# A smaller set-up product, a divided last store and later softmax steps in a TensorE-bound kernel

## The chip, the cores and the metric

The kernel runs on one core of one Trainium2 chip. The metric is the device time of one execution in microseconds (us), given as the median of several runs. The profile covers one execution; its "span", from the first to the last instruction, is some 1.8 us shorter than the metric.

## The reference

A dynamic convolution (7 taps, weights by softmax from `weight_gen`, 8 heads) is followed by a maxout layer:

```python
# attention part: x (8, 4160, 192), weight_gen (8, 4160, 8 heads, 7 taps)
w = softmax(weight_gen, axis=-1)                  # with a padded window of 7 tokens
out = einsum('bshk,bskhg->bshg', w, x_unfolded)   # -> (33280, 192)
# maxout part, w1 and w2 (192, 1024), w_out (1024, 192)
g = np.maximum(x @ w1, x @ w2)
return g @ w_out                                  # float32
```

## The kernel before

The kernel uses max(h1, h2) = h1 + relu(h2 - h1). So the output is `y @ (w1 @ w_out) + relu(y @ (w2 - w1)) @ w_out`. The small matrix `w10 = w1 @ w_out` (192 x 192) is computed once at the start, on the chip: w1 is transposed on TensorE (`tp`), copied to SBUF (`w1t`), multiplied by `wo` (`pw`), and copied to `w10`. Two output columns share 384 transposed rows, that is three slices of 128, so `w10` is kept in three slices: rows 0 to 127, rows 64 to 191, and rows 128 to 191 followed by 0 to 63.

The parts that the change touches (cuts marked):

```python
w1t = pstage.tile([P, FCH * 256], BF16, name="w1t")
def w1_transposed():
    tp = ...
    for fi in range(FCH):                                   # 8 blocks, 3 transposes each
        for at, kind, nr in ((0, "E", P), (P + 64, "E", 64), (P, "T", 64)):
            nc.tensor.matmul(tp[:, fi * 256 + at:...], lhsT=w1[kind][...], rhs=ident[...], is_transpose=True, ...)
    for h in range(2):
        nc.scalar.copy(out=w1t[:, h * 1024:(h + 1) * 1024], in_=tp[:, h * 1024:(h + 1) * 1024])
...
def w10_product():
    pw = ...
    for k in range(3):                                      # 3 x 8 products of 192 columns
        for fi in range(FCH):
            nc.tensor.matmul(pw[:, k * 256:k * 256 + D],
                lhsT=w1t[:, fi * 256 + 64 * k:fi * 256 + 64 * k + P], rhs=wo[:, fi * D:(fi + 1) * D], ...)
    nc.scalar.copy(out=_sub(w10, 0, [[D, 3], [1, D]]), in_=_sub(pw, 0, [[256, 3], [1, D]]))
...
hidden(1); w1_transposed(); ln(1); shift(1)                 # order of issue in the set-up (cut)
hidden(2); weights(1, 0); weights(1, 4); ...; exp_sum(2); sum_transpose(2); ...
hidden(3); w10_product(); sum_transpose(3); ...; out_rests(3, 0)    # out_rests uses w10 first (L275)
```

The last pair of output columns is copied from PSUM by one ScalarE instruction of 384 columns (line 305) and stored by one transfer (line 312). In the steady part, `extra(t)` issues ln, exponentials (`weights`, `exp_sum`), VectorE's multiplications and additions at fixed tiles of a batch of 16. At the very start, until its first data arrive, TensorE runs 115 warm-up products (`warm`, line 504) whose result nobody uses.

The softmax here doesn't subtract the row's maximum and nothing guards it: scores larger than these inputs give would overflow.

Of the kernel before, what the change touches and what calls it, by code (L numbers as in the profile page):

```python
# [10 lines left out]
BF16 = mybir.dt.bfloat16  # L11
# [6 lines left out]
def _sub(base: bass.AP, off: int, dims):  # L18
    ap = [list(base.ap[0])] + [[int(s), int(c)] for s, c in dims]
    return dataclasses.replace(base, offset=base.offset + off, ap=ap)  # L20
# [3 lines left out]
def kernel(  # L24
# [9 lines left out]
    nc = tc.nc  # L34

    B, S, D = x.shape
    H, K = weight_gen.shape[2], weight_gen.shape[3]
    F = moe_w1.shape[1]
    P = 128
    PAD = K - 1  # L40
    WGC = H * K
    FCH = F // P
    CPP = B * S // P
# [6 lines left out]
    NB = len(BATCHES)  # L50


    def pieces(b):
        n = BATCHES[b][1]
        at, done = [], 0
        for w in {0: (4, 4, 4, 4), 1: (4, 4, 8)}.get(b, (8, 8) if n == 16 else (n,)):
            at.append((done, w))
            done += w
        return at
# [8 lines left out]
    NT = len(TILES)  # L68
# [54 lines left out]
    def exp_sum(b):  # L123
        e_ts[b] = pe_.tile([P, BATCHES[b][1] * WGC], FP32, name="e_t", tag="e")
        nc.scalar.activation(out=e_ts[b], in_=wg_ts[b], func=AF.Exp)  # L125

    def red(b):
        TH = BATCHES[b][1] * H
        s_ts[b] = psm.tile([P, TH], FP32, name="sum_t", tag="sum")
        nc.vector.reduce_sum(out=s_ts[b], in_=_sub(e_ts.pop(b), 0, [[K, TH], [1, K]]), axis=AX.X)  # L130

    def ln(b):
        nc.scalar.activation(out=s_ts[b], in_=s_ts[b], func=AF.Ln)

    def shift(b):
        TH = BATCHES[b][1] * H
        w_t = _sub(wg_ts[b], 0, [[K, TH], [1, K]])
        nc.vector.tensor_tensor(out=w_t, in0=w_t, in1=_sub(s_ts.pop(b), 0, [[1, TH], [0, K]]),
                                op=ALU.subtract)

    def weights(b, o):

        N = dict(pieces(b))[o] * H
        if b not in en_ts:
            en_ts[b] = pen.tile([P, 16 * WGC * 2], BF16, name="en_t", tag="en")
        nc.scalar.activation(  # L146
            out=_sub(en_ts[b], o * WGC * 2, [[2 * N, K], [2, N], [1, 2]]),
            in_=_sub(wg_ts[b], o * WGC, [[1, K], [K, N], [0, 2]]), func=AF.Exp,
        )


    def mul(b, o):

        n = dict(pieces(b))[o]
        if b not in m_ts:
            m_ts[b] = pm.tile([P, K * 16 * D], BF16, name="m_t", tag="m")
        nc.vector.tensor_tensor(  # L157
            out=m_ts[b][:, K * o * D:K * (o + n) * D],
            in0=_sub(xb_ts[b], o * D, [[D, K], [1, n * D]]),
            in1=_sub(en_ts[b], o * WGC * 2, [[2, K * n * H], [0, G // 2], [1, 2]]),  # L160
            op=ALU.mult,
        )

    def adds(b, o):

        w = dict(pieces(b))[o]
        n = w * D
        m_t = m_ts[b]

        def taps(at, step, cnt):  # L170
            return _sub(m_t, K * o * D + at * n, [[step * n, cnt], [1, w * D]])

        if b not in y_ts:
            y_ts[b] = py.tile([P, 16 * D], BF16, name="y_t", tag="y")
        nc.vector.tensor_tensor(out=taps(0, 1, 3), in0=taps(0, 1, 3), in1=taps(3, 1, 3), op=ALU.add)  # L175
        nc.vector.tensor_tensor(out=taps(0, 2, 2), in0=taps(0, 2, 2), in1=taps(1, 5, 2), op=ALU.add)  # L176
        nc.vector.tensor_tensor(out=y_ts[b][:, o * D:(o + w) * D],  # L177
                                in0=taps(0, 1, 1), in1=taps(2, 1, 1), op=ALU.add)

    def transpose(u):  # L180

        b, o, n = UNITS[u]
        yt = pyt.tile([P, 8 // 2 * 3 * P], BF16, name="yt", tag="yt")
        nc.sync.dma_start_transpose(
            out=yt[:, 0:n // 2 * 3 * P].rearrange("p (b t) -> p b t", t=P),
            in_=y_ts[b][:, o * D:(o + n) * D],
        )
        yt_ts[u] = yt

        c = b + 1 if o == 0 else b + 2  # L190
        if u > 5 and c < NB:
            nc.gpsimd.tensor_copy(out=gate, in_=yt[:, 0:1])  # L192
            if o == 8:
                load_x(c, 0, min(8, BATCHES[c][1]))
            else:
                if BATCHES[c][1] > 8:
                    load_x(c, 8, BATCHES[c][1] - 8)
                if b + 3 < NB:
                    load_wg(b + 3, nc.gpsimd)
# [18 lines left out]
    rd_at, hd_at, op_at, o_t = {}, {}, {}, []  # L218
# [40 lines left out]
    def column(c):  # L259

        b = min(c // 16, NB - 1)
        for u, (ub, o, n) in enumerate(UNITS):
            if ub == b and o <= c - BATCHES[b][0] < o + n:
                k = c - BATCHES[b][0] - o
                return u, k // 2, k % 2
# [32 lines left out]
    def evac(p, n):  # L298

        tile_, at = op_at[p]  # L300
        k = 2 * p % 24
        m = min(n, 12 - k // 2)
        for q, w in ((0, m), (m, n - m)):
            if w:
                nc.scalar.copy(out=_sub(o_t[0], (k + 2 * q) % 24 * D, [[2 * D, w], [D, 2], [1, D]]),  # L305
                               in_=_sub(tile_, at + q * D, [[D, w], [512, 2], [1, D]]))
        for q in range(p, p + n):
            u, i, _ = column(2 * q)
            w = 1 if u == NU - 1 else UNITS[u][2] // 2
            if i % w == w - 1:  # L310
                k = 2 * (q + 1 - w)
                nc.scalar.dma_start(
                    out=bass.AP(tensor=out.tensor, offset=k * D, ap=[[CPP * D, P], [1, 2 * w * D]]),
                    in_=o_t[0][:, k % 24 * D:(k % 24 + 2 * w) * D],
                )
# [3 lines left out]
    OUTS, c = [], 0  # L319
# [73 lines left out]
    w10 = consts.tile([P, 3 * D], BF16, name="w10")  # L393
# [5 lines left out]
    with tc.tile_pool(name="pstage", bufs=1) as pstage:  # L399
# [7 lines left out]
        for p0, p1, eng in ((16, P, nc.sync), (1, 16, nc.gpsimd)):  # L407
            eng.dma_start(
                out=xs[p0:p1, 0:PAD * D],
                in_=bass.AP(tensor=x.tensor, offset=(p0 * CPP - PAD) * D,  # L410
                            ap=[[CPP * D, p1 - p0], [1, PAD * D]]),
# [38 lines left out]
        for o in (0, 4, 8, 12):  # L450
            weights(0, o)
        nc.vector.tensor_copy(out=xb_ts[0][:, PAD * D:(PAD + 4) * D],
                              in_=xs[:, PAD * D:(PAD + 4) * D])
# [5 lines left out]
        def w_diff(h, copy):  # L459
# [15 lines left out]
            out=wo[:, :].rearrange("p (f d) -> p f d", d=D),  # L475
            in_=bass.AP(tensor=moe_w_out.tensor, offset=0, ap=[[D, P], [P * D, FCH], [1, D]]),
# [3 lines left out]
        load_x(1, 8, 8)  # L480
        load_wg(3, nc.gpsimd)

        w1t = pstage.tile([P, FCH * 256], BF16, name="w1t")

        def w1_transposed():

            tp = ps["o"].tile([P, 1024], FP32, name="tp", tag="op")[:, :].bitcast(BF16)
            for fi in range(FCH):
                for at, kind, nr in ((0, "E", P), (P + 64, "E", 64), (P, "T", 64)):
                    nc.tensor.matmul(  # L490
                        tp[:, fi * 256 + at:fi * 256 + at + nr],
                        lhsT=w1[kind][0:nr, fi * P:(fi + 1) * P],
                        rhs=ident[0:nr, 0:nr], is_transpose=True, skip_group_check=True,
                    )
            for h in range(2):
                nc.scalar.copy(out=w1t[:, h * 1024:(h + 1) * 1024],
                               in_=tp[:, h * 1024:(h + 1) * 1024])

        warm = ps["h"].tile([P, 1024], FP32, name="warm", tag="hd")

# [27 lines left out]
        def w10_product():  # L528

            pw = ps["o"].tile([P, 1024], FP32, name="pw", tag="op")  # L530
            for k in range(3):
                for fi in range(FCH):
                    nc.tensor.matmul(  # L533
                        pw[:, k * 256:k * 256 + D],
                        lhsT=w1t[:, fi * 256 + 64 * k:fi * 256 + 64 * k + P],
                        rhs=wo[:, fi * D:(fi + 1) * D],
                        start=(fi == 0), stop=(fi == FCH - 1), skip_group_check=True,
                    )
            nc.scalar.copy(out=_sub(w10, 0, [[D, 3], [1, D]]), in_=_sub(pw, 0, [[256, 3], [1, D]]))


        hidden(2)
# [37 lines left out]
    def extra(t):  # L580

        u, k = TILES[t]
        b, o, n = UNITS[u]
        s = o + k
        if s == 0 and b + 1 < NB:

            c = b + 1
            if c + 1 < NB:
                red(c + 1)
            mul(c, 0)  # L590
            adds(c, 0)
        if s == 1 and b + 2 < NB:
            ln(b + 2)
            shift(b + 2)
            mul(b + 1, 8)
            adds(b + 1, 8)
        if k == 2 and 6 < u + 1 < NU:
            transpose(u + 1)
        if b + 2 < NB:
            for o, at in zip((o for o, _ in pieces(b + 2)), (12, 15)):  # L600
                if s == at:
                    weights(b + 2, o)
        if s == 9 and b + 3 < NB:
            exp_sum(b + 3)

    for g in range(3, len(OUTS)):
        if GROUPS[min(g, len(GROUPS) - 1)][1] == 3 and "c" not in ps:
# [51 lines left out]
```

## Time and profile before

| | before |
|---|---|
| time, first three runs | 428.1 us (427.99 to 428.15) |
| span of the profiled execution | 425.9 us (this execution took 427.68 us) |
| first hidden product (line 237) | 15.15 us |
| first use of `w10` (line 275) | 32.93 us, 17.78 after it |
| end of the last product of TensorE | 422.13 us |
| from there to the end | 3.76 us |

Read it as three lengths: a start that ends with the first hidden product, a body that TensorE fills almost without a gap, and a tail of copy, store and final checks. The body is 422.13 - 15.15 = 406.98 us. Any gain inside the body must show as an earlier first use of `w10`, since the steady part repeats at a fixed pitch after it.

### The profile page before, as it was taken

The page shows a single profiled execution, that of the slowest core. Times are in us where ns is not written, and L with a number is a line of the kernel's source. Part 1 is how long each engine was busy: PE and PEld are TensorE (multiplying, and loading weights), DVE is VectorE, ACT ScalarE, POOL GpSimd, SP SyncE. Part 2 cuts the span into 40 slices and gives each one's busy share as a digit, 9 for nine tenths or more (in the row PEclk, how much of TensorE's full clock was granted, in tenths as well). Part 3 has the DMA queues.
Part 4 walks back from the last instruction along what each step waited for, and adds up shares of the span by engine and source line. Part 5 has one row for each costly group of instructions (what it writes and reads, how often), then busy time and mean ns, then how long its engine had stood idle before and what let it go on. Part 6 is the DMA issues. An engine that isn't in the chain of part 4 may idle for free.

```text
span 425.9 us, 9277 instructions
## 1 busy us (share of the span) xinstructions
PE 418.4 (98%) x4139; PEld 300.2 (70%) x4139; DVE 381.8 (90%) x176; ACT 351.5 (83%) x353; POOL 81.5 (19%) x101
## 2 busy tenths in 40 slices
PE   7999999999999999999999999999999999999996
PEld 7889876666776767766667767667666677676685
DVE  6989999999999999999999999999999999997000
ACT  5896889898888979788898979898887988787762
POOL 1510032323112213221201131130222113110000
PEclk9999999999999999999999999999999999999999
DMA  8994256585675656667776667666766566644112
GB/s 253 252 233 93 76 145 150 86 198 168 169 191 112 202 130 184 159 130 192 175 193 124 161 159 184 138 165 179 178 154 182 96 162 149 154 115 131 75 75 111
DMA packets 62167, 65.85 MB, mean 155 GB/s; under 512 B 49937, under 2 KB 50577, under 8 KB 62128
## 3 DMA queue, kind: packets, MB, share of 16 engines
q0 software_dynamic: 8128, 24.11, 27.0%
q1 hardware_dynamic: 48672, 15.59, 18.7%
q10 hardware_dynamic: 5328, 25.56, 15.4%
q8 instruction: 32, 0.52, 0.5%
q14 instruction: 7, 0.06, 0.0%
HBM read 35.96 MB, written 25.56 MB: 144 GB/s over the span
## 4 chain that ended last, share of the span: by engine, by line
PE 94%; ACT 3%; DMA 2%; SPq 1%; issue 0%
PE op_ps L292 40%; PE hd L237 27%; PE hd L247 14%; PE op_ps L282 5%; PE op_ps L275 3%; PE yps L208 2%; DMA xs<-in_x_dram 2%; PE hdp L237 1%; ACT rd_t L256 1%; PE hdp L247 1%; PE tp L490 1%; SPq L426 1%; PE pw L533 0%; ACT en_t L146 0%; ACT o_t L305 0%; ACT xb_t L455 0%
## 5 line engine op out<-in xcount | busy, mean ns | idle before, releaser
L256 ACT ACTIVATE rd_t<-hd 128x2048 bf16<-128x2048 f32 (+1 forms) x166 | 230.9, 1445 | 33.1 <-PE hd L247 32.6
L292 PE MATMUL op_ps<-wo,rd_t 128*128 128x192 bf16 x2080 | 200.2, 246 | 0.0
L157 DVE TENSOR_TENSOR m_t<-xb_t,en_t 128x10752 bf16<-128x10752 bf16 (+1 forms) x36 | 187.3, 5206 | 1.7 <-ACT en_t L146 1.5
L292 PEld LDWEIGHTS <-rd_t 128*128 128x128 bf16 x2080 | 175.6, 98 | 9.2
L192 POOL CAST gate<-yt 128x1 f32<-128x1 bf16 x28 | 45.8, 1635 | 278.9 <-DMA yt<-y_t 278.9
L237 PE MATMUL hd<-yt,wdE 128*128 128x512 bf16 (+1 forms) x264 | 96.5, 370 | 0.2 <-ACT rd_t L256 0.2
L237 PE MATMUL hd<-yt,wdO 128*128 128x512 bf16 (+1 forms) x264 | 95.5, 366 | 0.0
L175 DVE TENSOR_TENSOR m_t<-m_t 128x4608 bf16<-128x4608 bf16 (+1 forms) x31 | 76.9, 2480 | 1.1
L305 ACT COPY o_t<-op_ps 128x384 f32<-128x384 f32 (+1 forms) x89 | 56.1, 630 | 25.9 <-PE op_ps L292 23.8
L247 PE MATMUL hd<-yt,wdR 64*128 64x512 bf16 (+1 forms) x528 | 68.0, 366 | 0.0
L282 PE MATMUL op_ps<-w,yt 128*128 128x192 bf16 x260 | 64.0, 246 | 0.0
L176 DVE TENSOR_TENSOR m_t<-m_t 128x3072 bf16<-128x3072 bf16 (+1 forms) x31 | 52.9, 1706 | 1.1
L247 PEld LDWEIGHTS <-wdR 64*128 64x128 bf16 x576 | 20.8, 94 | 44.8 <-issue 35.0
L237 PEld LDWEIGHTS <-wdE 128*128 128x128 bf16 x288 | 28.0, 97 | 29.0 <-issue 19.2
L146 ACT ACTIVATE en_t<-wg_t 128x896 bf16<-128x896 f32 (+1 forms) x36 | 34.2, 960 | 2.1 <-ACT o_t L305 2.1
L237 PEld LDWEIGHTS <-wdO 128*128 128x128 bf16 x288 | 28.2, 98 | 10.4 <-issue 0.7
L282 PEld LDWEIGHTS <-yt 128*128 128x128 bf16 x260 | 25.4, 98 | 9.6 <-issue 0.3
L177 DVE TENSOR_TENSOR y_t<-m_t 128x1536 bf16<-128x1536 bf16 (+1 forms) x31 | 28.9, 932 | 1.1
L275 PE MATMUL op_ps<-w,yt 64*128 64x192 bf16 x260 | 25.2, 243 | 0.2 <-ACT o_t L305 0.2
L275 PEld LDWEIGHTS <-yt 64*128 64x128 bf16 x260 | 12.8, 94 | 14.6 <-issue 0.7
L130 DVE TENSOR_REDUCE sum_t<-e_t 128x128 f32<-128x896 f32 (+1 forms) x17 | 17.6, 1038 | 2.3 <-ACT e_t L125 2.3
L125 ACT ACTIVATE e_t<-wg_t 128x896 f32<-128x896 f32 (+1 forms) x17 | 15.7, 925 | 3.9 <-DMA wg_t<-in_weight_gen_dram 2.3
(51 smaller groups left out, 161.7 us busy)
## 6 DMA issues: line engine op xcount, KB each, us to landing
out_dram<-o_t ACTq DMA_DIRECT2D x29, 768.0 KB, 3.8
xb_t<-in_x_dram POOLq DMA_DIRECT2D x28, 384.0 KB, 4.7
wg_t<-in_weight_gen_dram POOLq DMA_DIRECT2D x14, 448.0 KB, 5.1
xb_t<-xb_t POOLq DMA_DIRECT2D x16, 288.0 KB, 5.0
out_dram<-o_t ACTq DMA_DIRECT2D x6, 384.0 KB, 2.6
wg_t<-in_weight_gen_dram SPq DMA_DIRECT2D x2, 448.0 KB, 5.2
xs<-in_x_dram SPq DMA_DIRECT2D x2, 384.0 KB, 6.4
xb_t<-in_x_dram POOLq DMA_DIRECT2D x1, 768.0 KB, 10.4
```

What stands on the lines that cost most here:

```text
L146: nc.scalar.activation(out=_sub(en_ts[b], o * WGC * 2, [[2 * N, K], [2, N], [1, 2]]), in_=_sub(wg_ts[b], o * WGC, [[1, K], [K, N], [0, 2]] ...
L157: nc.vector.tensor_tensor(out=m_ts[b][:, K * o * D:K * (o + n) * D], in0=_sub(xb_ts[b], o * D, [[D, K], [1, n * D]]), in1=_sub(en_ts[b], o ...
L175: nc.vector.tensor_tensor(out=taps(0, 1, 3), in0=taps(0, 1, 3), in1=taps(3, 1, 3), op=ALU.add)
L176: nc.vector.tensor_tensor(out=taps(0, 2, 2), in0=taps(0, 2, 2), in1=taps(1, 5, 2), op=ALU.add)
L192: nc.gpsimd.tensor_copy(out=gate, in_=yt[:, 0:1])
L237: nc.tensor.matmul(hid_out(t, f, j), lhsT=wd[kind][:, f * P:(f + 1) * P], rhs=_sub(yt_ts[u], 2 * j * P, [[3 * P, w // P], [1, P]]), start= ...
L247: nc.tensor.matmul(hid_out(t, f, j), lhsT=wd["R"][r, f * P:(f + 1) * P], rhs=_sub(yt_ts[u][r, :], P, [[3 * P, w // P], [1, P]]), start=fir ...
L256: nc.scalar.activation(out=rd[:, k * 1024:(k + n) * 1024], in_=hd[:, at:at + n * 1024], func=AF.Relu)
L275: nc.tensor.matmul(op_out(c), lhsT=yt_ts[u][r, (3 * i + 1) * P:(3 * i + 2) * P], rhs=w10[r, 2 * D:3 * D], start=first, stop=False, skip_gr ...
L282: nc.tensor.matmul(op_out(c), lhsT=yt_ts[u][:, (3 * i + 2 * j) * P:(3 * i + 2 * j + 1) * P], rhs=w10[:, j * D:(j + 1) * D], start=False, s ...
L292: nc.tensor.matmul(op_out(c), lhsT=rd[:, k * 1024 + at:k * 1024 + at + P], rhs=wo[:, f * D:(f + 1) * D], start=False, stop=(f == FCH - 1), ...
L305: nc.scalar.copy(out=_sub(o_t[0], (k + 2 * q) % 24 * D, [[2 * D, w], [D, 2], [1, D]]), in_=_sub(tile_, at + q * D, [[D, w], [512, 2], [1, ...
```

## The change

Its intent: fewer TensorE instructions in the set-up (8 transposes and 8 products of the 24 each were repetitions of rows that exist already), the last two columns evacuated and stored side by side by two engines, and softmax steps placed some tiles later in a batch. The diff, with cuts marked by "...":

```diff
@@ evac @@
+        if p == NT // 2 - 1:
+            for j, copy, eng in ((0, nc.scalar.copy, nc.scalar), (1, nc.vector.tensor_copy, nc.sync)):
+                copy(out=o_t[0][:, (k + j) * D:(k + j + 1) * D], in_=tile_[:, at + j * 512:at + j * 512 + D])
+                eng.dma_start(out=... column 2 * p + j ..., in_=o_t[0][:, (k + j) * D:(k + j + 1) * D])
+            return
@@ w1_transposed @@
-        w1t = pstage.tile([P, FCH * 256], BF16, name="w1t")
+        w1t = pstage.tile([P, FCH * D], BF16, name="w1t")
-                for at, kind, nr in ((0, "E", P), (P + 64, "E", 64), (P, "T", 64)):
+                o = fi // 4 * 1024 + fi % 4 * D
+                for at, kind, nr in ((0, "E", P), (P, "T", 64)):
...
@@ w10_product @@
-            for k in range(3):
+            for at, c0, nr in ((0, 0, P), (512, P, 64)):
                 for fi in range(FCH):
...
-            nc.scalar.copy(out=_sub(w10, 0, [[D, 3], [1, D]]), in_=_sub(pw, 0, [[256, 3], [1, D]]))
+            for k, to, frm, at in ((0, 0, 0, 0), (1, 0, 64, 0), (2, 64, 0, 0), (1, 64, 0, 512),
+                                   (2, 0, 0, 512)):
+                nr = P if k == 0 else 64
+                nc.scalar.copy(out=w10[to:to + nr, k * D:(k + 1) * D],
+                               in_=pw[frm:frm + nr, at:at + D])
@@ extra @@
-        if s == 1 and b + 2 < NB:
+        if s == 4 and b + 2 < NB:
             ln(b + 2)
...
-            for o, at in zip((o for o, _ in pieces(b + 2)), (12, 15)):
-                if s == at:
-                    weights(b + 2, o)
+        for o, at in ((0, 14), (8, 17)):
+            c = (t - at) // 16 + 2
+            if (t - at) % 16 == 0 and 2 < c < NB and o in dict(pieces(c)):
+                weights(c, o)
...
```

More of the change, by code (lines that the diff above doesn't have):

```diff
@@ L301, in evac @@
         k = 2 * p % 24
+        if p == NT // 2 - 1:
+            for j, copy, eng in ((0, nc.scalar.copy, nc.scalar), (1, nc.vector.tensor_copy, nc.sync)):
+                copy(out=o_t[0][:, (k + j) * D:(k + j + 1) * D], in_=tile_[:, at + j * 512:at + j * 512 + D])
+                eng.dma_start(
+                    out=bass.AP(tensor=out.tensor, offset=(2 * p + j) * D, ap=[[CPP * D, P], [1, D]]),
+                    in_=o_t[0][:, (k + j) * D:(k + j + 1) * D],
+                )
+            return
         m = min(n, 12 - k // 2)
@@ L488, in w1_transposed @@
             for fi in range(FCH):
-                for at, kind, nr in ((0, "E", P), (P + 64, "E", 64), (P, "T", 64)):
+                o = fi // 4 * 1024 + fi % 4 * D
+                for at, kind, nr in ((0, "E", P), (P, "T", 64)):
                     nc.tensor.matmul(
-                        tp[:, fi * 256 + at:fi * 256 + at + nr],
+                        tp[:, o + at:o + at + nr],
                         lhsT=w1[kind][0:nr, fi * P:(fi + 1) * P],
@@ L495, in w1_transposed @@
             for h in range(2):
-                nc.scalar.copy(out=w1t[:, h * 1024:(h + 1) * 1024],
-                               in_=tp[:, h * 1024:(h + 1) * 1024])
+                nc.scalar.copy(out=w1t[:, 4 * h * D:4 * (h + 1) * D],
+                               in_=tp[:, h * 1024:h * 1024 + 4 * D])
         warm = ps["h"].tile([P, 1024], FP32, name="warm", tag="hd")
@@ L530, in w10_product @@
             pw = ps["o"].tile([P, 1024], FP32, name="pw", tag="op")
-            for k in range(3):
+            for at, c0, nr in ((0, 0, P), (512, P, 64)):
                 for fi in range(FCH):
                     nc.tensor.matmul(
-                        pw[:, k * 256:k * 256 + D],
-                        lhsT=w1t[:, fi * 256 + 64 * k:fi * 256 + 64 * k + P],
+                        pw[0:nr, at:at + D], lhsT=w1t[:, fi * D + c0:fi * D + c0 + nr],
                         rhs=wo[:, fi * D:(fi + 1) * D],
@@ L598, in extra @@
             transpose(u + 1)
-        if b + 2 < NB:
-            for o, at in zip((o for o, _ in pieces(b + 2)), (12, 15)):
-                if s == at:
-                    weights(b + 2, o)
-        if s == 9 and b + 3 < NB:
-            exp_sum(b + 3)
+        for o, at in ((0, 14), (8, 17)):
+            c = (t - at) // 16 + 2
+            if (t - at) % 16 == 0 and 2 < c < NB and o in dict(pieces(c)):
+                weights(c, o)
+        c = (t - 9) // 16 + 3
+        if (t - 9) % 16 == 0 and 3 < c < NB:
+            exp_sum(c)
     for g in range(3, len(OUTS)):
```

## The prediction

> **What bounds the kernel now.** I read the page first (busy time, 40 slices, chain), then the table of windows, then the timeline of the stretch that the change edits, then the last microseconds.
>
> ```profile
> PE 418.4 (98%) x4139; PEld 300.2 (70%) x4139; DVE 381.8 (90%) x176; ACT 351.5 (83%) x353; POOL 81.5 (19%) x101
> ...
> PE 94%; ACT 3%; DMA 2%; SPq 1%; issue 0%
> ...
> 44.00:52.00 8.00, 7.57 (x88) 6.19 (x86) 7.90 (x6) 6.70 (x8) 0.00 (x0) 1.00 0.28 81
> ...
> 132.00:204.00 72.00, 72.00 (x673) 49.49 (x672) 71.38 (x31) 62.03 (x61) 16.11 (x18) 1.00 0.66 162
> ...
> 419.00:426.00 7.00, 3.13 (x38) 2.90 (x36) 0.00 (x0) 1.66 (x3) 0.00 (x0) 1.00 0.43 169
> ```
>
> Columns of a window: length, then busy us (instructions) of PE, PEld, DVE, ACT, POOL, then clock, DMA share, GB/s. TensorE is without a gap for 72 us in the steady stretch, at full clock, and is 94% of the chain. Busy can mislead, so I checked the pitch: two groups of three tiles take 9.01 us again and again (from 91.45 to 100.46, 109.47, 118.49 and so on in the chain), always the same. So after some 52 us only a change in the number of TensorE instructions, or a new wait of TensorE, can move the end. VectorE is nearly as full (71.38 of 72) but runs ahead. Three places are left: the ramp, the tail, and the question whether moved ScalarE work makes TensorE wait.
>
> The ramp, from the timeline (start, us, engine line):
>
> ```profile
> 23.21 1.93 ACT L496 COPY w1t<-tp 128x1024 bf16<-128x1024 bf16 x2 [0.52 <-PE tp L490]
> 23.66 1.08 DVE L130 TENSOR_REDUCE sum_t<-e_t 128x128 f32<-128x896 f32 x1
> 25.03 0.32 ACT L133 ACTIVATE sum_t<-sum_t 128x128 f32<-128x128 f32 x1
> 28.51 2.14 PE L533 MATMUL pw<-wo,w1t 128*128 128x192 bf16 x24
> 29.57 1.98 ACT L256 ACTIVATE rd_t<-hdp 128x1024 bf16<-128x1024 f32 x2
> 30.49 2.51 PE L208 MATMUL yps<-ident,m_t 128*128 128x128 bf16 x42
> 31.39 0.69 ACT L539 CAST w<-pw 128x576 bf16<-128x576 f32 x1
> 32.93 0.34 PE L275 MATMUL op_ps<-w,yt 64*128 64x192 bf16 x4
> ```
>
> Look at who is late here: TensorE is busy throughout, but ScalarE also runs without a gap from 25.03 to 32.08. The copy of w10 is done at 32.08, 0.85 us before its first user, the product of line 275 at 32.93. That 0.85 us is all the room there is.
>
> The tail, and three 64-partition copies that I use as a scale:
>
> ```profile
> 422.16 0.48 ACT L305 COPY o_t<-op_ps 128x384 f32<-128x384 f32 x1 [1.01 <-PE op_ps L292]
> 422.67 0.34 ACTq L312 DMA_DIRECT2D out_dram<-o_t  x1
> ```
> ```profile
> 12.39 0.62 ACT L464 COPY wdR<-wdE 64x512 bf16<-64x512 bf16 x1
> 13.02 0.62 ACT L465 COPY wdO<-wdE 64x512 bf16<-64x512 bf16 x1
> 13.66 0.62 ACT L468 COPY wdO<-wdR 64x512 bf16<-64x512 bf16 x1
> ```
>
> **What the skill says.** (1) The Trainium skill, "TensorE: Matmul & The Clock Gate", section "Back-to-back issue gap": N/2.4 + 2.5 ns for an isolated warm product, so 82.5 ns at N = 192. The trace agrees: 24 products fill 28.51 to 30.49, 1.98 / 24 = 82.5 ns. (2) "VectorE: DVE Perf Modes", section on the TRN2 errata: out of PSUM a ScalarE operation takes (172 + N) and a VectorE one (120 + N) cycles at 1.2 and 0.96 GHz. ScalarE's 384 columns give 463 ns by it, the trace has 0.48 us, so I trust it to 4%. No VectorE copy out of PSUM is in the trace. (3) "ScalarE: Activation LUTs", section "What ACT_TABLE_LOAD costs": back-to-back ACTIVATEs overlap by about 93 ns. The trace agrees for full-width ones (the two w1t copies, 1.93 us together), but the three copies above, 64 partitions each and to other partitions, start 0.63 and 0.64 us apart at 0.62 us each: no overlap. (4) "DMA: Bandwidth & Descriptors", section "Issuing engines are not separate DMA queues": issuing from two engines only saves the issue time. Here that is 0.34 us.
>
> **The change part by part.**
>
> *Transposes.* 8 of 24 go, those of 64 rows that stood directly before another one of 64 rows. In the start times of the trace such a neighbour costs 0.03 to 0.04 us (the switch from 128 to 64 rows, about 0.16 us, stays): 8 x 0.035 = 0.28 us. The two copies of w1t shrink from 1024 to 768 columns, 2 x 256 x 0.83 ns = 0.43 us of ScalarE. The ln after them cannot use all of it: it needs the sum that VectorE ends at 24.74. So ln goes from 25.03 to about 24.78, and the ScalarE row behind it moves 0.25 us ahead.
>
> *Products.* 24 become 16 of the same 192 columns: 8 x 82.5 ns = 0.66 us less on TensorE. Together TensorE could be 0.94 us earlier at 32.93, that is at 31.99.
>
> *Copies of w10.* One of 0.69 us becomes five of 192 columns. One is (172 + 192) / 1.2 = 303 ns, by the trace's 4% rather 0.32. Four of them are on 64 partitions, three shifted. Without overlap: 5 x 0.33 = 1.65 us; with an overlap of 0.1 each: 1.25 us. They start when the two relus before them are done, so at 31.39 - 0.25 = 31.14, and end at 32.4 to 32.8. TensorE's first use follows some 0.05 us later: 32.45 to 32.85 instead of 32.93. So the room of 0.85 us is used up, TensorE waits 0.45 to 0.85 us of the 0.94 it won, and **0.1 to 0.5 us stays**; I take 0.3.
>
> *Tail.* The intent is that the second column's copy and store run beside the first's. The built program's list of waits says otherwise: both copies wait for the same last count of TensorE, and the VectorE copy waits for the ScalarE copy besides. So from the last product at 422.13: ScalarE 0.32 us, to 422.49; 0.08 for the hand-over; VectorE (120 + 192) / 0.96 = 325 ns, to 422.90; SyncE issues at 422.93, against 422.67 now: 0.26 later. The store is half as large (96 KB; the groups of stores have 2.1 us for 192 KB and 2.6 for 384 KB, so some 0.1 to 0.2 less), and one check less stands behind it at the end (0.06). Net: about **+0.05 us**, from -0.05 to +0.15.
>
> *Softmax later.* The ln goes from tile 1 to 4 of a batch, the exponentials from 12 and 15 to 14 and 17. VectorE's order is unchanged.
>
> ```profile
> 314.44 1.08 DVE L130 TENSOR_REDUCE sum_t<-e_t 128x128 f32<-128x896 f32 x1
> ```
> ```profile
> 315.84 0.34 ACT L133 ACTIVATE sum_t<-sum_t 128x128 f32<-128x128 f32 x1
> ```
>
> Here the ln starts only 0.32 us after its sum is ready. A batch takes VectorE 24.08 us (shifts at 61.52, 85.60) and TensorE 24.03, so this margin melts, and with TensorE some 0.3 us earlier ScalarE would begin to wait. The move prevents that: it gains nothing by itself. What it spends is lead of en_t over VectorE's multiplication. Placing each moved instruction behind its new relu in the old timeline, the least lead is about zero for batch 3 (VectorE may wait up to 0.6 us once, near 74.5) and 0.3 to 2 us later. TensorE's lead over this is larger: the transpose of a unit is issued 7.5 us or more before its first use, and lands after 4.3 in the median. So 0 us.
>
> Sum: -0.3 + 0.05 = -0.25 us; 428.1 becomes 427.85, say **427.8**.
>
> **Rivals.** *A: the whole TensorE saving arrives.* 0.94 us less, 427.2. For it: TensorE is the chain's owner. Against it: the gapless ScalarE row and the five copies. It needs copies that overlap strongly. *B: the copies eat it all*, and the serial tail costs more than I think (two starts instead of one, VectorE slow out of PSUM): 428.1 to 428.4. For it: the copies of line 464 don't overlap. *C: the moved softmax stalls VectorE often*, and units arrive late on TensorE: each batch could lose up to a microsecond, 430 or more. Against it: the 7.5 us of lead, which melts by only 0.05 us a batch. *D: the tail works as intended*, both columns side by side: about 0.2 us less than my figure, 427.6.
>
> **Range and chances.** A and D together give 427.0, B gives 428.4; the three runs of before lie within 0.16 us. Range 427.0 to 428.5. A change of 2% is 8.6 us; no part touches more than a microsecond, so faster 0.005, slower 0.01 (only C), same 0.985.
>
> **What would show it.** In the changed profile: 16 products in 1.32 us and 16 transposes in some 2.3; five copies of w10 filling 1.25 to 1.65 us from about 31.1; a new wait of the line 275 product on ScalarE of 0.45 to 0.85 us, and none after; VectorE's copy after, not beside, ScalarE's, and the last store issued 0.2 to 0.3 us later after the last product than before; ln with 5 us between sum and start; steady groups still at 9.01 us. I am wrong if that wait is absent (A), if the two last copies run side by side (D), or if TensorE waits on yt (C).

## The result, and the profile after

The changed kernel took 427.57 us in the median (427.52 to 427.92, 4 runs), against 428.05 us for the kernel before (427.70 to 428.15, 4 runs) on the same chip. The ratio is 0.9992, with a 95% interval of 0.9975 to 1.0009. Class: same. The output is correct. The prediction of 427.8 us and "same" held. The interval includes 1, and it is wider than the 0.25 us that was predicted, so the time alone proves nothing about the parts.

The page of the kernel after, busy time per engine and the head of the chain that ended last:

```profile
PE 418.5 (98%) x4123; PEld 300.1 (70%) x4123; DVE 382.3 (90%) x177; ACT 352.1 (83%) x357; POOL 84.3 (20%) x101
...
PE 96%; ACT 2%; issue 0%; DVE 0%; POOL 0%; POOLq 0%; DVEq 0%
```

Sixteen products of TensorE and their weight loads are gone (4139 to 4123 of each), and yet its busy time did not fall. The chain is still TensorE's. Two windows of the kernel after, the steady stretch and the end:

```profile
132.00:204.00 72.00, 72.00 (x674) 49.34 (x672) 71.38 (x31) 62.17 (x60) 13.98 (x16) 1.00 0.66 163
419.00:426.00 7.00, 2.99 (x36) 2.76 (x34) 0.36 (x1) 1.35 (x3) 0.00 (x0) 0.96 0.44 169
```

Nothing moved in the steady stretch, as expected; the groups of six tiles follow each other at 9.01 us as before (91.31, 100.32, 109.33). In the end window VectorE now has its one copy (0.36 us).

The timeline of the set-up after (start, us, engine line, as in the prediction):

```profile
23.52 1.50 ACT L506 COPY w1t<-tp 128x768 bf16<-128x768 bf16 x2 [0.30 <-PE tp L500]
23.57 1.08 DVE L130 TENSOR_REDUCE sum_t<-e_t 128x128 f32<-128x896 f32 x1
...
24.91 0.32 ACT L133 ACTIVATE sum_t<-sum_t 128x128 f32<-128x128 f32 x1
...
28.82 1.60 PE L543 MATMUL pw<-wo,w1t 128*128 128x192 bf16 x16
...
31.25 1.55 ACT L551 CAST w<-pw 128x192 bf16<-128x192 f32 x5
...
32.86 0.34 PE L275 MATMUL op_ps<-w,yt 64*128 64x192 bf16 x4
```

The first use of `w10` came at 32.86 instead of 32.93, only 0.07 us earlier. The five copies fill 31.25 to 32.80, and the product follows 0.06 us behind the last. Between ln (24.91) and first use lie 7.95 us, filled by ScalarE throughout. The weight loads of the eight 64-column products begin only after a gap of 0.16 us; it returns in e9.

But TensorE shows no wait at line 275 in this profile, and the reason is a second thing that has nothing to do with the change. Here is the window from 7 to 9 us, first of the kernel before, then of the kernel after; the second number and its count are TensorE's warm-up products:

```profile
7.00:9.00 2.00, 2.00 (x36) 2.00 (x34) 1.70 (x3) 2.00 (x4) 0.00 (x0) 1.00 1.02 318
```

```profile
7.00:9.00 2.00, 2.00 (x22) 2.00 (x20) 1.79 (x3) 1.99 (x4) 0.00 (x0) 1.00 1.07 325
```

The same instruction passes 36 times in one and 22 times in the other. (The clock column says 1.00 in both; here the count tells it, not the column.) By the pitch of these products, which falls from 107 to 56 ns, TensorE went to full speed at 7.30 us before and at 9.03 us after. The fixed 115 warm-up products therefore ended at 11.63 us before and 12.45 after, and the first hidden product came at 15.69 us instead of 15.15: TensorE began its body 0.54 us late. So the body shrank by 406.98 - 406.30 = 0.68 us, but 0.54 of that only made good the late start, and the last product ended 0.14 us earlier (421.99).

The tail of the kernel after:

```profile
422.02 0.32 ACT L305 COPY o_t<-op_ps 128x192 f32<-128x192 f32 x1 [1.00 <-PE op_ps L292]
...
422.43 0.36 DVE L305 COPY o_t<-op_ps 128x192 f32<-128x192 f32 x1 [29.92 <-ACT o_t L305]
422.82 0.36 SPq L306 DMA_DIRECT2D out_dram<-o_t  x1
```

VectorE's copy begins only when ScalarE's is done (its releaser is named in the bracket), so the last store is issued 0.83 us after the last product, against 0.54 before. The store then lands 1.64 us after its issue instead of 1.87, being half as large, and the last checks take 1.29 instead of 1.35. The tail is 3.76 us in both kernels.

In the steady part ln now has its room: in the batch that the prediction showed, it starts 4.51 us after the end of its sum (321.12 - 315.53 - 1.08), not 0.32. VectorE's wait for the later exponentials occurs once, and is larger than I thought:

```profile
315.53 1.08 DVE L130 TENSOR_REDUCE sum_t<-e_t 128x128 f32<-128x896 f32 x1
...
321.12 0.33 ACT L133 ACTIVATE sum_t<-sum_t 128x128 f32<-128x128 f32 x1
```

```profile
75.64 5.76 DVE L157 TENSOR_TENSOR m_t<-xb_t,en_t 128x10752 bf16<-128x10752 bf16 x1 [1.12 <-ACT en_t L146]
```

TensorE does not notice it: its only waits of more than 0.1 us after 40 us, at 45.1 and 50.8, are 0.2 us each in both kernels.

### The profile page after: what moved, and what is told of

It reads as the page before. It is cut to its first block, busy times and chain, and to the rows that moved or that the text cites. A ratio compares the mean times of both kernels' runs of the same rounds, so it can differ in the third digit from the quotient of the medians.

```text
span 425.7 us, 9249 instructions
## 1 busy us (share of the span) xinstructions
PE 418.5 (98%) x4123; PEld 300.1 (70%) x4123; DVE 382.3 (90%) x177; ACT 352.1 (83%) x357; POOL 84.3 (20%) x101
## 3 DMA queue, kind: packets, MB, share of 16 engines
q1 hardware_dynamic: 48816, 15.69, 19.7%
## 4 chain that ended last, share of the span: by engine, by line
PE 96%; ACT 2%; issue 0%; DVE 0%; POOL 0%; POOLq 0%; DVEq 0%
PE op_ps L292 40%; PE hd L237 27%; PE hd L247 14%; PE op_ps L282 5%; PE yps L208 3%; PE op_ps L275 3%; PE warm L514 2%; PE hdp L237 1%; ACT rd_t L256 1%; PE hdp L247 1%; PE tp L500 1%; ACT en_t L146 0%; PE pw L543 0%; ACT o_t L314 0%; ACT yt L214 0%
## 5 line engine op out<-in xcount | busy, mean ns | idle before, releaser
L192 POOL CAST gate<-yt 128x1 f32<-128x1 bf16 x28 | 49.2, 1756 | 280.2 <-DMA yt<-y_t 280.2
```

The source lines that it names most:

```text
L192: nc.gpsimd.tensor_copy(out=gate, in_=yt[:, 0:1])
```

## The experiments

Theory: ScalarE's row from ln to the copies of `w10` sets the first use of `w10`, so TensorE's saving is mostly eaten by the five copies; the tail is serial because of a wait between the two copies; the softmax move is free and useless here. Main rival: the copies are hidden, TensorE sets the first use, and what is missing was lost elsewhere (softmax, or the late clock). The number that tells them apart is the time from the first hidden product (h) to the first use of `w10`, since it leaves out where TensorE began.

| run | median us (n) | before | first use - h | body | tail |
|---|---|---|---|---|---|
| before | 428.05 (4) | | 17.78 | 406.98 | 3.76 |
| after | 427.57 (4) | 428.05 | 17.17 | 406.30 | 3.76 |
| e1_w10_only | 427.74 (4) | 427.66 | 17.69 | 406.86 | 3.82 |
| e2_tail_only | 428.06 (4) | 427.66 | 17.79 | 406.97 | 3.75 |
| e3_soft_only | 427.83 (4) | 427.66 | 17.78 | 406.90 | 3.75 |
| e4_copies_twice | 429.07 (4) | 427.66 | 19.17 | 409.91 | 3.86 |
| e5_tail_split | 427.12 (4) | 427.96 | 17.22 | 406.35 | 3.31 |
| e6_w10_early | 427.23 (4) | 427.96 | 17.12 | 406.25 | 3.75 |
| e7_warm_85 | 427.63 (4) | 427.96 | 17.69 | 406.94 | 3.75 |
| e8_all | 427.69 (6) | 427.96 | 17.12 | 406.54 | 3.30 |
| e9_four_copies | 427.23 (4) | 427.98 | 17.21 | 406.35 | 3.74 |
| e10_best | 426.57 (6) | 427.98 | 16.89 | 406.03 | 3.31 |
| e11_best_nosoft | 426.37 (6) | 427.98 | 16.89 | 406.09 | 3.29 |
| e12_before_early | 427.59 (4) | 427.98 | 17.78 | 406.96 | 3.75 |

All outputs are right. Kernels are compared only within the same rounds. The last three columns are from one profiled execution each.

**e1_w10_only.** The kernel before with the hunks of `w1_transposed` and `w10_product` alone.

> Only the w10 part of the change (16 transposes, 16 products, five copies). From the first hidden product (line 237) to the last product the kernel before took 406.98 us and the changed one 406.30. My theory, that this part alone makes the difference: 406.3, within 0.1. Rival, that the moved softmax contributes: 406.6 or more here, or new waits of ScalarE on VectorE's sums (the ln of batches 8, 11, 14) that TensorE feels. The part from the last product to the end: 3.76 us. The time itself depends on when TensorE's clock is let go at the start: 7.30 us in the trace of before, 9.03 in the changed one; if it is late, the first hidden product is 0.5 us late.

Measured: 427.74 us, ratio 1.0000 (0.9985 to 1.0015). Here h was at 15.43 us and VectorE's sum ended at 25.15, so both ran 0.3 to 0.4 us behind the kernel before, and the first use of `w10` came 17.69 us after h: 0.09 less. This is the new wait, in the timeline:

```profile
33.12 0.34 PE L275 MATMUL op_ps<-w,yt 64*128 64x192 bf16 x4 [0.51 <-ACT w L542]
```

TensorE stood 0.51 us for the copies, and first use followed ln by 33.12 - 25.18 = 7.94 us, as after the whole change (7.95). So the w10 part by itself keeps only 0.1 us. My expectation failed here: the body is 406.86 and not 406.3, and from 406.6 up I had meant to see a share of the softmax move in it. But that move alone leaves the body at 406.90 (e3), and e7 has all parts of the change and a body of 406.94. The 406.30 of the profile after was short because TensorE began it late, not because of another part.

**e2_tail_only** and **e3_soft_only.** The kernel before with the hunk of `evac` alone, and with the hunk of `extra` alone.

> Only the last two columns by two engines. Theory: the VectorE copy runs after ScalarE's, so the last store is issued some 0.83 us after the last product instead of 0.55, the smaller store and one check less give it back, and the part from the last product to the end stays at 3.76 us, within 0.05. Rival, that the two engines help: 3.5 us or less. First hidden product to last product: 406.98, as before.

> Only the softmax moves. Theory: no time; first hidden product to last product 406.98 within 0.05, tail 3.76; the ln starts some 5 us after its sum in every batch, and VectorE waits once for en_t, near 75 us, by up to 1 us. Rival: ScalarE's queue with the old places delayed relus, and the move gains 0.2 us or more.

Measured: 428.06 (ratio 1.0007, 0.9992 to 1.0022) and 427.83 (1.0006, 0.9989 to 1.0023). Tails of 3.75 us and first uses of 17.79 and 17.78: neither part moves anything by itself. VectorE waits once in e3, 1.10 us near 75 us.

**e4_copies_twice.** The changed kernel, each copy of `w10` written twice.

```diff
-            for k, to, frm, at in ((0, 0, 0, 0), ...):
+            for k, to, frm, at in 2 * ((0, 0, 0, 0), ...):
```

> The changed kernel with the five copies of w10 done twice over (same result). Theory: the copies end when TensorE needs them, so they are on the path: the five more cost 1.55 us, TensorE's first product with w10 comes 1.5 us later than in the changed kernel (17.17 us after the first hidden product there, 18.7 here), and the end comes 1.4 to 1.5 us later. Rival, that there is room left: less than 0.7 us later.

Measured: 429.07 us (428.70 to 430.50), ratio 1.0037 (1.0020 to 1.0055), the only clear slowdown. The copies and the wait, from the timeline, and a window behind it:

```profile
31.07 3.01 ACT L551 CAST w<-pw 128x192 bf16<-128x192 f32 x10
...
34.12 0.38 PE L275 MATMUL op_ps<-w,yt 64*128 64x192 bf16 x4 [1.98 <-ACT w L551]
```

```profile
34.00:36.00 2.00, 1.88 (x14) 1.60 (x14) 1.93 (x3) 1.89 (x4) 0.00 (x0) 0.58 0.04 18
```

Five more copies cost 1.5 us and the first use came 1.48 us later than with five (19.17 against 17.69 in e1; ln stood 9.75 us behind h in both). So first use follows the copies one to one: the rival that they are hidden falls. (I had expected 18.7, counted from the 17.17 of the kernel after, in which TensorE hardly waited.) In this profiled run there is more: the clock column of the window says 0.58, and also 0.57 from 36 to 38, which makes (0.42 + 0.43) x 2 / 0.5 = 3.4 us at half speed, behind a wait of 2 us. That run took 430.5 us, the three others 428.7 to 429.1 at a granted clock of 0.999 to 1.000. That the wait caused it is not shown: one run of the kernel before, which has no such wait in its profile, took 431.07 us at 0.996, the figure of this run.

**e5_tail_split.** The changed kernel, the last two columns in PSUM tiles of their own and the first of them in an SBUF tile of its own; VectorE and SyncE take the first column while TensorE computes the second.

```diff
-            for j, copy, eng in ((0, nc.scalar.copy, nc.scalar), (1, nc.vector.tensor_copy, nc.sync)):
-                copy(out=o_t[0][...], in_=tile_[:, at + j * 512:at + j * 512 + D])
+            for c, o, copy, eng in ((2 * p, o_t[1], nc.vector.tensor_copy, nc.sync),
+                                    (2 * p + 1, o_t[0][:, (k + 1) * D:(k + 2) * D], nc.scalar.copy, nc.scalar)):
+                out_col(c)
+                copy(out=o, in_=op_out(c))       # op_out(c) is now a PSUM tile of that column alone
```

> The changed kernel with the last two columns each in a PSUM tile of its own (the slots of r and ab, free by then), the first copied by VectorE into a tile of its own and stored by SyncE while TensorE computes the second, which ScalarE copies and stores. In the built program VectorE's copy then waits for its own products alone. Theory: what made the two copies queue was the shared tiles; the last copy (0.32 us) and its store are issued 0.39 us after the last product instead of 0.83, so from the last product to the end 3.3 us instead of 3.76. Rival, that the stores themselves or the order of their semaphores set the end: 3.6 us or more.

Measured: 427.12 us, ratio 0.9979 (0.9961 to 0.9998). The tail fell from 3.76 to 3.31 us:

```profile
421.36 0.36 DVE L310 COPY o_last<-op_r 128x192 f32<-128x192 f32 x1 [28.85 <-PE op_r L296]
...
422.03 0.32 ACT L310 COPY o_t<-op_ab 128x192 f32<-128x192 f32 x1 [1.30 <-PE op_ab L296]
422.38 0.34 ACTq L311 DMA_DIRECT2D out_dram<-o_t  x1
```

VectorE now waits for the products of its own column, not for ScalarE, and is finished before the last product ends. Two variants were built and not run. With only the SBUF tile divided, the list of waits still held VectorE behind ScalarE's last copy; with only the PSUM tile divided, that wait was gone. So, by these lists, the wait that made the changed tail serial belongs to the shared PSUM tile. What this fix gains is 0.45 us, of which 0.15 is the earlier last issue (0.39 us after the last product against 0.54 before); the rest is about what the smaller store and the shorter checks gained in the kernel after (0.23 and 0.06).

**e6_w10_early.** The changed kernel, `w10_product()` ahead of the fourth hidden tile.

```diff
-        hidden(3)
         w10_product()
+        hidden(3)
         sum_transpose(3)
```

> The changed kernel with the w10 products one place earlier, ahead of the hidden products of group 3 instead of behind them, so that on ScalarE the five copies stand ahead of that group's two relus. Theory: the copies are then done at about 31.0 us, a microsecond before their first use, TensorE sets that use itself, at 16.9 us after the first hidden product (17.17 in the changed kernel, 17.78 before), about 7.2 us after the ln of batch 1 instead of 7.95, and the saved 0.9 us reaches the end: 0.5 to 0.9 us less span than the changed kernel. Rival A: ScalarE's row is only reordered and the copy of yt or a relu becomes the wait: first use unmoved. Rival B: the gain is lost later, on VectorE's lead: first use earlier, last product not.

Measured: 427.23 us, ratio 0.9980 (0.9965 to 0.9996). The copies now stand ahead of the two relus:

```profile
29.14 1.52 ACT L551 CAST w<-pw 128x192 bf16<-128x192 f32 x5
...
32.46 0.34 PE L275 MATMUL op_ps<-w,yt 64*128 64x192 bf16 x4
```

They are done at 30.66, 1.8 us before the first use, which comes 17.12 us after h without any wait. That is TensorE's own limit with this change: 0.66 us less than before, and 0.57 less than in e1. It is less than I expected: 17.12 and not 16.9 from h, and a span 0.41 us below that of the kernel after and not 0.5 to 0.9. I had still counted 0.94 us of TensorE saving; it is 0.68, as worked out below.

**e7_warm_85.** The changed kernel with 85 warm-up products instead of 115, so that TensorE begins when its data is there.

> The changed kernel with 85 instead of 115 warm-up products ahead of the first sum. In the trace of the changed kernel the clock was let go at 9.03 us and the warm-up ended at 12.45, 0.9 us after its successor's data were there (11.47); with the clock let go at 7.3 it ended at 11.63. Theory: with 85 the first sum starts at its data (about 11.5 after a first exponential at 4.29) whenever the clock comes, the first hidden product at about 15.15; but as ScalarE's row from ln on sets the use of w10, the end moves by no more than 0.15 us. Rival: the whole start depends on it, 0.5 us less on average, or the gap before the first sum makes the clock fall back and costs 1 us or more.

Measured: 427.63 us (427.57 to 428.64). With TensorE no longer late the wait at line 275 is there, 0.51 us, and the first use 17.69 us after h, both as in e1. So the missing wait in the profile of the kernel after was TensorE's late start. No time is won, as ScalarE's row doesn't begin earlier. One run of four took 1 us longer at a lower granted clock (0.995).

**e8_all.** The changes of e5, e6 and e7 together.

> The changed kernel with all three: own tiles for the last columns, w10 earlier, 85 warm-up products. If the three causes are independent their gains add up: about 0.45 + 0.75 + 0.1, so span 424.4 us against 425.75 of the changed kernel and 425.89 of before, and a median near 426.3 us, 0.3 to 0.4% faster than before. If VectorE's lead runs out it is less, and then TensorE shows waits on yt.

Measured: 427.69 us where I expected 426.3, six runs in two groups: 426.73, 426.87 and 427.05 at a clock of 0.999 to 1.000, and 428.33, 428.38 and 428.44 at 0.995. In the profile TensorE now stands 1.8 us for its first data behind the 85 warm-up products. Half of the runs thus lose what the edits of e5 and e6 win. The fewer warm-up products are the likely cause, since e7, which has them too, has one run of four at 0.995, and e10, with 115, has none of six. But the profiled run was one of the good ones, so where the clock is lost in the others is not shown. The good runs miss the sum of the gains too: in the profiled one h came at 15.43 us, behind a wait of 0.55 us for `yt`.

**e9_four_copies.** The changed kernel, the second half of the product with 128 columns of `w1t` (rows 64 to 191 of w1), so that slice 1 of `w10` is one full copy.

```diff
-            for at, c0, nr in ((0, 0, P), (512, P, 64)):
+            for at, c0 in ((0, 0), (512, 64)):           # always P columns of w1t from c0
...
-            for k, to, frm, at in ((0, 0, 0, 0), (1, 0, 64, 0), (2, 64, 0, 0), (1, 64, 0, 512),
-                                   (2, 0, 0, 512)):
+            for k, to, nr, frm, at in ((0, 0, P, 0, 0), (1, 0, P, 0, 512), (2, 0, 64, 64, 512), (2, 64, 64, 0, 0)):
```

> The changed kernel, but the second half of the w10 products keeps 128 columns (rows 64 to 191 of w1), so that the second slice of w10 lies ready in one 128-row copy: four copies instead of five, and no switch to 64-column products. Theory (ScalarE's row sets the first use of w10, a copy costs 0.3 us of it): first use of w10 follows ln by about 7.6 us instead of 7.95; block of 16 products 1.32 us instead of 1.54; with TensorE's start as in the kernel before, first use 17.3 to 17.4 us after the first hidden product instead of 17.69. Span and median 0.2 to 0.35 us below the changed kernel. Rival (w10 is no longer what TensorE waits for): no difference from the changed kernel.

Measured: 427.23 us, ratio 0.9979 (0.9952 to 1.0006). In the timeline:

```profile
31.15 1.22 ACT L549 CAST w<-pw 128x192 bf16<-128x192 f32 x4
...
32.42 0.34 PE L275 MATMUL op_ps<-w,yt 64*128 64x192 bf16 x4 [0.25 <-ACT w L549]
```

First use follows ln (24.79) by 7.63 us instead of 7.95, and the wait halves to 0.25 us. By start times the 16 products take 1.32 us from the first to what follows them, where the changed kernel takes 1.53 for as many. The difference lies at the border from 128 to 64 columns and back: 0.176 and 0.178 us there, in place of 0.083. First use is at 17.21, somewhat better than the 17.3 to 17.4 I expected.

**e10_best** and **e11_best_nosoft.** e10 is the changed kernel with the edits of e5, e6 and e9 and all 115 warm-up products. e11 is the same with the softmax steps where they were before.

> The changed kernel with the two improvements that held (w10 product ahead of the fourth hidden tile; last two columns in PSUM tiles of their own) and the four copies; warm-up products left at 115. Theory: TensorE-bound up to the first use of w10, which comes 16.9 us after the first hidden product (17.12 before minus 0.22 for the switch to 64 columns); tail 3.3 us. Median 426.6 to 426.9, ratio 0.9965 to 0.998. Rival (four copies bring nothing more once the product is early): 427.0.

> The same with ln and the exponentials at their old places. In the profile of the kernel before ln of some batches had only 0.3 to 0.6 us left after its sum. Theory 1 (the later places only keep the room that a faster TensorE would use up): ScalarE waits a few tenths of a us on VectorE's sum once or twice, TensorE at most 0.1, so time as with the later places within 0.1 us. Theory 2 (they are needed): 0.3 us or more slower than with the later places.

Measured: 426.57 us (426.24 to 428.18), ratio 0.9969 (0.9944 to 0.9993), and 426.37 us (426.14 to 426.55), ratio 0.9957 (0.9935 to 0.9979). In both the first use of `w10` is 16.89 us after h, as worked out beforehand (16.9).

That is 0.89 us less than before, and the tail is 0.45 us shorter. Together 1.34 us; the span fell by 425.89 - 424.50 = 1.39. (One of e10's runs took 428.18 us at a clock of 1.0; why is not known.) The two kernels do not differ as far as six runs each can tell, and bodies of 406.03 and 406.09 say the same: the later softmax places are not needed. What they were there for does show in e11, in the batch that the prediction pointed at:

```profile
315.21 0.31 ACT L133 ACTIVATE sum_t<-sum_t 128x128 f32<-128x128 f32 x1 [0.28 <-DVE sum_t L130]
```

ScalarE waits 0.28 us there for the sum, and 0.13 us at 242.95; TensorE's waits are the same 0.2 and 0.2 us as everywhere.

**e12_before_early.** The kernel before with the order of e6 only.

> The kernel before, only with its w10 product ahead of the fourth hidden tile. Theory: in the kernel before TensorE, not the copy of w10, sets the first use of w10 (17.78 us after the first hidden product), so moving the product changes nothing: 17.75 to 17.85, ratio 0.999 to 1.001. If the gain of the same order in the changed kernel came from the order itself (and not from letting 0.66 us of removed products through), this run would be 0.4 us or more faster.

Measured: 427.59 us, ratio 0.9987 (0.9955 to 1.0019), and first use 17.78 us after h, unchanged to the hundredth, though the copy now ends 1.9 us earlier (30.17 instead of 32.08). So the order by itself gives nothing; it only lets through what the removed products save.

## Why the prediction was right

The class, the value (427.57 against 427.8) and the range held. The mechanism held too, in the executions in which TensorE begins on time (e1, e7). That the value came so near is partly luck: 0.25 us less was forecast, the medians fell by 0.48, the two profiled spans by 0.14, and the forecast rested on a TensorE saving and a kept share that were both too large. Point by point:

- **The bound.** TensorE without gaps, and only the ramp and the tail open to change: right. In every experiment but e4 the body changed by what the first use of `w10` changed, within 0.1 us, except e8 (0.2). In e4 the body grew by 1.5 us more, about what 3.4 us at half speed cost.
- **Transposes, -0.28 us.** The block of transposes went from 2.58 to 2.35 us by start times, -0.23. Right to 0.05: the eight neighbours that went had cost 39 to 40 ns each, as read, but the switch back to 128 rows, 122 ns before, is 132 ns now.
- **Products, -0.66 us.** The mechanism was right, the size off: 1.98 to 1.53 us, so -0.45. I counted eight instructions less of 82.5 ns and overlooked that eight of the rest are of 64 columns, with two borders of 0.09 us. e9 without them took the full 1.32 us that the prediction named. TensorE's possible saving was 0.23 + 0.45 = 0.68, which e6 shows as 0.66, not 0.94.
- **ln, -0.25 us.** Only 0.12 in the profile after (25.03 to 24.91), as TensorE's late start also delayed the transposes and the copies of `w1t`, which ended at 25.02. With TensorE on time it is VectorE's sum that binds, as predicted: in e7 the sum ends at 24.82 and ln starts at 24.86.
- **Five copies, 1.25 to 1.65 us.** 1.55 us, all but one of the copies without overlap. The prediction took the middle of its range, the chip gave nearly the upper end; this (0.10 us) and the smaller advance of ln (0.13 us in the profile after) are why 0.07 to 0.09 us was kept in place of 0.3. The room of 0.85 us was indeed all there was.
- **TensorE's wait at line 275, 0.45 to 0.85 us.** It is absent in the profile after, which the prediction named as a sign of rival A. It is not: e1 and e7 show it with 0.51 us, and it was missing because TensorE itself was 0.54 us late in that execution. (e5, with h at 15.64 us, lacks it too: 0.03 us.) The sign was badly chosen, for it depends on when TensorE begins; the time from ln to first use (7.94 to 7.95 us in after, e1 and e7) would have been the firm one.
- **Tail, +0.05 us.** 0.00. Each term held nearly: issue 0.29 later (0.26 said), store 0.23 less (0.1 to 0.2 said), checks 0.06 less. The serial order read from the list of waits was right, and rival D fell.
- **Softmax, 0 us.** Right for TensorE. VectorE's single wait was 1.12 us in that profile, where I had said up to 0.6, and 1.10 in e3; in e10 it was 0.48. It ends with an exponential of ScalarE; why it was about twice the estimate was not looked into. Rival C fell.

The median came down by 0.48 us and the span by 0.14, because the two profiled executions do not stand alike in their groups: they took 427.68 us (before) and 427.56 us (after), so the one of before is 0.4 us faster than its median and the one of after is at it. The medians of before (427.66, 427.96, 427.98) differ among themselves by 0.3 us, so a part of the 0.48 is scatter; how much of it is real stays open.

Where TensorE's saving goes when TensorE begins on time is settled: into ScalarE's copies, as e1, e4 and e6 show from three sides. In the profiled execution of the kernel after, most of it made good the late start instead.

## What to carry to other kernels

A saving on the busiest engine is worth only what the next row in line leaves of it: before cutting instructions, measure how long the other engine's product has been ready when it is first used (0.85 us here), and if the cut lengthens that engine's row, move the work ahead in its queue (e6) or shorten it (e9). If two engines are to copy side by side, look in the list of waits for a tile that they share; the one that counted here was in PSUM. And compare lengths from a fixed event inside the body: the moment at which TensorE comes to full speed moved by 3 us from run to run and hid in one profile the very wait that was predicted.

## What the Trainium skill lacked or had wrong

- "TensorE: Matmul & The Clock Gate", section "LDWEIGHTS (loading the stationary operand)": it puts the load's time in ns at the number of columns over 1.2, which gives 107 ns for 128 and 53 for 64. The 128-column loads of `w1t` took 98 ns and the 64-column loads 106 to 110.
- The same page, "Back-to-back issue gap": it gives some 81 ns as the sustained spacing at 128 columns with a load for each. The 42 products of line 208, a load each, follow one another at 55.8 ns, as its formula for isolated ones says. And no page that I read has the border between 128- and 64-column products: 0.18 us in place of 0.083, each way.
- The same page, "Part 1: The HAM clock gate": it gives the moment of full speed as about 4 us of activity, give or take 0.5. Counted from the first warm-up product at 3.0 us, it came 2.9 us (e2) to 6.0 us (after) later. It also names about 3.4 us of idling before the clock falls; in e4's profiled run it fell 0.18 us after a wait of 1.98 us had ended (34.30 us in the trace's clock record). A wait of 1.82 us in e8's profiled run passed without a fall, and e4's other runs show a clock of 0.999 to 1.000, so no length of wait can be read from this.
- "VectorE: DVE Perf Modes", section on the TRN2 errata: its formula gives an estimate of 325 ns for a VectorE copy of 192 columns out of PSUM; the trace has 358.
- "ScalarE: Activation LUTs", "What ACT_TABLE_LOAD costs": the overlap of 93 ns doesn't hold for every pair. Of the five copies of `w10`, only the fourth overlaps its forerunner (pitch 0.22 us; the others 0.32 to 0.38), and it is the one that reads and writes the same partitions as that. In e9 the pair of full copies overlaps too, and the two shifted ones don't. In e4 the sixth copy overlaps the fifth (0.22 us) as well: both start at partition 0 on both sides, with 128 and 64 partitions. Every pair that overlaps also reads from the other half of `pw` (column 0 against 512), as one pair in e9 that doesn't overlap does; so equal first partitions may be needed, alone or together with the other half. No run was made to part the two.
